# Two attention-and-FFN pairs prepared by halves of their heads, in a fused Trainium2 kernel with a fixed instruction order

## The chip, the cores and the metric

The kernel runs on one core of one Trainium2 chip. The metric is the time of the whole program on the device, in microseconds, as the median of several executions. A separate, profiled execution gives the trace and the profile page that this document reads. A core has a matrix engine (TensorE, PE in the profile; its weight loads are the row PEld), a vector engine (VectorE, DVE), a scalar engine (ScalarE, ACT), a general engine (GpSimd, POOL) and a sync engine (SyncE, SP) that issues most transfers.

## The reference, cut to what matters

Attention over four batches, eight heads, 768 positions and 64 values per head is followed by a gated feed-forward block. Three heads (0, 2 and 6) see all earlier keys; the other five see only four sink keys and a window of 64.

```python
scores = scale * q @ k.T                      # per batch and head, 768 x 768
keep   = causal & (retrieval_head | is_sink | in_window)
a      = softmax(where(keep, scores, -1e9))
x      = (a @ v) with heads side by side      # 3072 x 512
g      = x @ w_gate                           # 512 x 1536
out    = (g * sigmoid(g) * (x @ w_val)) @ w_out
```

Inputs and outputs are float32; the kernel computes its matrix products in float16 with float32 sums.

## The kernel before

The sequence is cut into 24 tiles of 128 queries, two tiles to a pair, twelve pairs. For each pair the kernel loads Q, K and V (512 KB each), casts Q and K to float16, turns them with PE transposes into a PSUM tile, and copies that tile out into `qT` and `kT`; later pairs (from the sixth on) are turned by DMA instead. Then each tile has a few score units (`sc`), an exponential for each (`ex`), the product with V (`val`), a division (`rc`, `nm`), and a transpose into `xt` (`xtr`, `xe`). Four tiles make a group, and each group has twelve column blocks of gate and value products (`gate`, `vals`), with a tanh on ACT and two instructions on DVE between them (`stt1`, `stt2`), and an output product (`out`).

Everything is a task with a name, the engines that may do it, and what it depends on. The order of all tasks and the engine of each are not found at run time: they are two long strings in the source, one for the order and one for the choices. Numbers from 3700 on in the order string are fillers: so many 512-column matmuls of the identity into a spare bank, whose result nobody reads.

```python
RINGS = {"raw": 14, "hq": 2, "e": 6, "xb": 3, "xt": 2, "sig": 2, "sil": 3,
         "h": 2 * NJ, "osb": 2, "gv": 3, "o": 1, "sc": 1, "av": 1, "tr": 1}
# "gv", "o", "sc", "av" and "tr" are PSUM; "tr" and "gv" tiles are one bank each

def recast(task, dst, src):              # float32 -> float16
    if task.way == "DVE":
        nc.vector.tensor_reduce(out=dst, in_=src.unsqueeze(len(src.shape)), ...)
    else:
        copy(task, dst, src)             # ACT or POOL

def cast(n, kd, x):                      # x is None from the third pair on
    r = landed[kd, n].rearrange("p (h j d) -> p h j d", j=2, d=64)
    ...
    if kd == "k":
        ks = slice(0, 2) if x is None else slice(x, x + 1)
        recast(T_c[n, kd, x], hqs[n][1][:, ks]..., r...[:, ks])
        return
    js = slice(0, 2) if x is None else slice(x, x + 1)      # odd or even rows
    recast(T_c[n, kd, x], hqs[n][0]...[:, :, :, js], r[:, :, js]...)

def transposes(n, w):                    # w: 0 for Q, 1 for K; eight transposes
    ring = "gv" if w and n < 2 else "tr"
    tr = buf(ring, [128, 4, 2, 2, 64] if w else [128, 2, 4, 128], FH, "tr")
    for j in range(2):
        for p in range(4):
            nc.tensor.transpose(...)
    trs[n, w] = tr

# ... for pairs 0 and 1, the copies of one PSUM tile in parts:
cut = [slice(2, 4), slice(0, 2)] if n < 2 else [slice(0, 4)]

def tasks_of_tile(t):
    ...
    k_deps = [x for kt in range(i // 2 + 1) for x in T_ev[QP.index((b, kt)), 2]]
    k_deps += T_ev[n, 0] + T_ev[n, 1]    # a score unit waits for all the parts
    for u, unit in enumerate(units):
        sc = P.add(f"sc{t}.{u}", ["PE"], ..., deps=k_deps + k_sinks + added,
                   takes=[score_ring(t, u)])
```

In the order string of this kernel the first loads are Q0, K0, Q1, V0, K1, Q2, V1, K2, then weights: two column blocks of the gate matrix (its second, then its first), and one of the value matrix.

Of the kernel before, what the change touches and what calls it, by code (L numbers as in the profile page):

```python
# [13 lines left out]


ORDER = (
    "080400091L1O021M1N01xh1T1U1W1V1Xxi1Y1a1Z1K0B0A1Rxm1t1u25261P0C280E031Q2D1r2G1S1s271n1d1o1b2E2j2I"
    "2F1e2H1i1c1f2K1p0D1q292A2J2L1g0F1y2p2k1h1j2M2C2r2q1v0j1w1k151x2V2Wxh2N1z202O2P0i0p1l2B1m2X2Z2a23"
    "242b2Yxh2Q2s9Z2R2S2c2t2T2d210H2U9j11309k312e9l109F0o2h2u9G162i9o9a9H9c2v0I0k0G9b9d3Q059e062x9f9p"
    "9q9m3W2y369n3D3Y9K0q9g22072z129I3E3X9J2f9N9L9M3A3B3M3R3Z3a9O189h2l2m9t9u9i2w3e9v9y0K329P333f9z9r"  # L20
    "9s34A00n350t3b2n37199w9x2o3C0m3cA13F3G1H3H3IA249134FAN3J4G9QAO9R3h9S9T3i3K1IAQ3g3pAP1E3z0s401FAS"
    "4HAR3d9UAV0J3S3TATAUAW3N9V3t380l3L3VAI0L9W3u1BAL3vAJ393j3k3l3mAKA8AM4A410N3n9X3o0r0O9Y3q4I423wA9"
    "3xA34o0M3U434J44ADAA4N3r4p3y3sAG453OAEAF0Q2g1CA44O4K4WABAH4q463P4L4BA54748A64Z4aBQ4MACA70xBTBR4c"
    "4l4dAwAx4vBS4CBU4xBf4PBg4DAyBh4Q4RBVBWAzBXB0ArAsB14bAtBiBj4S4w4TB24y5253B3B44U4VBGBH4z50B5BJBL5V"
    "0RBI4f0w5WBY4X4E4hBK5X1AB64gB75D4e5G5H0v17BZ1D510yB80u14BkAX5J4iB9BA0zBl4Y4j1J5K5fAY0PBM1GBNBm55"
    "4m564r54BaBEAZAa4k5L5d4s594t4u575A5cAu585B5E5eBb5g5hAvAc0T5CAdBc0bAe5I5Q5MBO0SBP5Z0UBB5N5O5RAfBC"
    "BDAhBd5P0VAi5S5TAjAb5oBFAk5pBnBeAg625Y634n64Bo5FAmAn5iAo5UCJ6761ApCd7SCKCL5r5s5tCeCf6BCgCh6ACsBp"
    "Bq5q5a68COCtCu5j7T5k695yAq656F5bCv5u7Q0X6i5v6GCPCQAlBr0W6g6CBs0a6O6p5w5x6DCwC95lCACB6ECMBuCR6UCS"
    "BvCNBwCn6V6I6hCoCpCb0Z6J6oBx6qBt0Y5zCY6kCZCaCcCT6X665m6Y6nBzCi6K6R6S7P0e6HC0C1Cl6LCjCkCmCCCUCV6M"
    "6d7W6uCD0g6T5n6v6NCE6P6w7XC260CHCxCFCGCI6rC46s7N6mC5Cy6z706Z6aCW6jCXCz6W6b6xCqC36QD08a6y7x6c6fCr"  # L30
    "6eC6C7By7O7VD2757U6tD37RD1787971D5D47AEF72E0E1E20c73D67B7C0hD7EDD876EGC87j7kEHEIEJEAEBECD9DA7D7g"
    "7t8i7l0d7vDRDB82DgDC7hEE7i7E7477DhDiE37m7n7z7FE5DSDTE6DDDEDF837GE47wE8Db7H6l7uE7E98eDUDVDcEK7I7Y"
    "7JENELEM7qEO7Z7aDHDIDd7KDe7LDq80817o0fDrDs7p877rDfDJ7yDKDWDXDYDt7b7cDu88DlDm847sDo8GDnDp857d8ZDv"
    "Dw8A7e8BDx89Dy8Y7MDM8JDG8KDjDzDk8LDN8MDZ7fEoEp8NFDFEDa868V8CFG8D8P8Q8c8E8gEqEjFFDOFH8dDPEkFIElDL"
    "EmFJ8f8h8pFL8FFKFMF88H8REP8qF9FA8jEn8k8bEQ8SEyEzFBERFC8m8lESETFS8xF0Et8nF18OEu8T8U9394F2EvEUEV8I"
    "ErEw8W8t8X90FTFUFcEW8oEx918r8uFdFe92FfEXDQ8sFX8v8wFg8y98EZFYEYEaFZ9996EsF3F495F58zEbEc979AF6FN9B"
    "9C9DEeEfF7FOFPFaFbFVEgFW9EGGEhGJEiGHGIGKGkGlGuGvGnGwGmFhFQGoGxGyFRG6G7FiFjFkFlEdG8GVGWGYGXGaG9Gb"
    "GcGZFmGpFnGqGrG1G2GAG3GsGBGtGCGdGeGDFoGLGMFpG4G5GQFrGRGSFsGTFtGOFuGNGfGgFvGPFqFwGhGEGFFxFyFzG0GU"
    "GiGzGjH0H1H4H2H3H5H6H7H8H9HAHBHEHFHCHDHGHHHJHIHKHL"
)  # L40
WAYS = (
    "000000000000000000000000000000000000000000000000000000000000002020222122002102002000012221100010"
    "001000000000100000000000000000101221222020011101100000000000000000000110022100001101001000000000"
    "100000100000000000002222220000100000100000000010000100100000000002022220110100000100000020000000"
    "100000010012202210000001001000000000100000010000000002221202000000000000000001000010022211210000"
    "000000000000220000001000000110202022000000000000000000000000000000000000012122000000000000000000"
    "010000210002221100000000010000001200010010000002001120011000000000000000000210000000000000000000"
    "000000000000000000000000000000000000000000000000000000000000000000000000000000000000000000000001"
    "000000000000000000000000000000000000000000000000000000000000000000000100001000000000000000000000"
    "000000000000000000000000000000000000000000000000000000000000000100000000000000000000000000000000"  # L50
    "000000000000000000000000000000000000010000100001000000000000000000000000000000000000000000000000"
    "000000000000000000000100000000000000000000000000000000000000000000000000000000000000000000000000"
    "10000000001000000010"
)
DIGITS = "0123456789ABCDEFGHIJKLMNOPQRSTUVWXYZabcdefghijklmnopqrstuvwxyz"

# [49 lines left out]
def kernel(  # L106
# [270 lines left out]
    def cast(n, kd, x):  # L377

        r = landed[kd, n].rearrange("p (h j d) -> p h j d", j=2, d=64)
        if n >= XQK and kd == "q":  # L380
            recast(T_c[n, kd, x],
                 hqz[:, :, x, :, x * 64:(x + 1) * 64].rearrange(
                     "p j (r k) d -> p k r j d", r=2),
                 r.rearrange("p (k s r) j d -> p s k r j d", r=2, s=2)[:, x])
            return
        if n not in hqs:
            h = buf("hq", [128, 2, 1024], FH, "hq")
            hqs[n] = [h[:, 0].rearrange("p (j r x) -> p j r x", j=2, r=2),
                      h[:, 1].rearrange("p (k a x) -> p k a x", k=2, a=4)]
        if kd == "k":  # L390
            ks = slice(0, 2) if x is None else slice(x, x + 1)
            recast(T_c[n, kd, x],
                 hqs[n][1][:, ks].rearrange("p k a (s d) -> p k s a d", s=2),
                 r.rearrange("p (k s r) j d -> p k s (r j) d", r=2, s=2)[:, ks])
            return
        js = slice(0, 2) if x is None else slice(x, x + 1)
        recast(T_c[n, kd, x],
             hqs[n][0].rearrange("p j r (k d) -> p k r j d", d=64)[:, :, :, js],
             r[:, :, js].rearrange("p (k r) j d -> p k r j d", r=2))

    def castv(n, m, j):
        b, pi = QP[n]
# [22 lines left out]

    trs = {}

    def transposes(n, w):

        ring = "gv" if w and n < 2 else "tr"  # L430
        tr = buf(ring, [128, 4, 2, 2, 64] if w else [128, 2, 4, 128], FH, "tr")
        for j in range(2):
            for p in range(4):
                if w:
                    nc.tensor.transpose(tr[:, p, :, j, :], hqs[n][1][:, p // 2, p % 2 * 2 + j],
                                        ident)
                else:
                    nc.tensor.transpose(
                        tr[:, j, p, :],
                        hqs[n][0][:, j, p // 2, (p % 2) * 128:(p % 2 + 1) * 128], ident)  # L440
        trs[n, w] = tr

    def evacq(n, s, x, ps):
        c = slice(s * 64, s * 64 + 64)
        copy(T_ev[n, s][x], qT[n % 2][c, s, ps].rearrange("c p j n -> c j p n"),
             trs[n, 0][c, :, ps])

    def evack(n, x, ps):


        b, pi = QP[n]
        copy(T_ev[n, 2][x],
             kT[b % 2][:, 2 * pi:2 * pi + 2].rearrange("c m k r x -> c (k r) m x")[:, ps],
             trs[n, 1][:, ps].rearrange("c p m j n -> c p m (j n)"))

    def sinks_k(b, m):

# [166 lines left out]
    def tasks_of_pair(n):  # L624
# [35 lines left out]
                deps=cs["k"] + older)) for m in range(2)]  # L660
            P.uses(first, "hq", *T_ev[n, 2])
        for w in range(xqk, 2 - xk):
            ring = "gv" if w and n < 2 else "tr"
            tr = P.add(f"tr{n}.{w}", ["PE"], (lambda n=n, w=w: transposes(n, w)),
                       deps=cs["qk"[w]], takes=[ring], after=[T_warm])
            cut = [slice(2, 4), slice(0, 2)] if n < 2 else [slice(0, 4)]
            evs = []
            if w:
                for x, ps in enumerate([slice(1, 4, 2), slice(0, 4, 2)] if n < 2 else cut):
                    evs.append(P.add(f"evk{n}.{x}", ["ACT", "DVE"],  # L670
                                     (lambda n=n, x=x, ps=ps: evack(n, x, ps)),
                                     deps=[tr] + older))
                T_ev[n, 2] = evs
            else:
                oldq = [x for t in (2 * n - 4, 2 * n - 3) if n > 1 for x in T_sc_of[TILES[t]]]
                T_ev[n, 0], T_ev[n, 1] = [], []
                for x, ps in enumerate(cut):
                    for s_ in range(2):
                        T_ev[n, s_].append(P.add(
                            f"evq{n}.{s_}{x}", ["ACT", "DVE"],  # L680
                            (lambda n=n, s_=s_, x=x, ps=ps: evacq(n, s_, x, ps)),
                            deps=[tr, T_fill0] + oldq))
                        evs.append(T_ev[n, s_][-1])
            P.uses(tr, ring, *evs)
            P.uses(first, "hq", tr)

    def tasks_of_tile(t):
        b, i = TILES[t]
        units = plan(t)
        n = t // 2  # L690
        k_deps = [x for kt in range(i // 2 + 1) for x in T_ev[QP.index((b, kt)), 2]]
        k_deps += T_ev[n, 0] + T_ev[n, 1]
        v_deps = [x for kt in range(i + 1) for x in T_v[QP.index((b, kt // 2)), kt % 2]]
        v_deps += [T_fill1]
        k_sinks = [T_sk[b, m] for m in range(1, i)]
# [5 lines left out]
        for u, unit in enumerate(units):  # L701
# [1 line left out]
            streams = any(kt < 0 or kt == i for p, hh, c, kt in mms if p)  # L703
            added = [T_masks[0 if t == 0 else 1]] if t < LEAD else []
            sc = P.add(f"sc{t}.{u}", ["PE"], (lambda t=t, u=u, unit=unit: scores(t, u, unit)),
                       deps=k_deps + k_sinks + added, takes=[score_ring(t, u)])
            T_sc_of[b, i].append(sc)
            if streams:
                own.append(sc)
# [223 lines left out]
```

The softmax here doesn't subtract the row's maximum and nothing guards it: scores larger than these inputs give would overflow.

## Time and profile before

| | before |
|---|---|
| time, median of 3 | 257.31 us (257.23 to 257.92) |
| span of the profiled execution | 255.5 us |
| PE busy | 246.7 us, 97% |
| DVE, ACT, POOL busy | 177.1, 135.3, 81.5 us |
| granted PE clock | 1.00 |
| filler matmuls of 512 columns | 21 |
| first gate product starts | 21.4 us |
| last matmul ends | 251.7 us |

The profile page has the busy time of each engine; the span in 40 slices; the transfers; the chain of work that ended last, which is followed back from the last instruction; and the costliest groups of instructions, with the idle time of the engine before them and what ended that idle time. The trace can also be asked for a timeline of one engine, and for a table of busy times by stretch. In a timeline each row is: start, duration, engine, source line, operation, what is written and read, shapes, how many instructions are merged into the row, and in brackets the idle time before it and what released it. Matmuls are pipelined: the 0.38 us of one 512-column matmul is its latency, and in a run of them one starts every 0.216 us (8 in 1.73 us). A busy PE is therefore not yet a PE at its peak, and 97% says little about what is left to win.

### The profile page before, as it was taken

How to read it: one execution, taken by the hardware profiler on the slowest of the kernel's cores; microseconds unless marked ns; L12 is line 12 of the kernel's file. 1: busy time of each engine (PE TensorE's matmuls, PEld its weight loads, DVE VectorE, ACT ScalarE, POOL GpSimd, SP SyncE). 2: the span in 40 equal slices, each digit the busy share in tenths (PEclk: the TensorE clock that was granted, in tenths of full speed). 3: DMA queues.
4: the chain of work that ended last, by engine and by line, in shares of the span. 5: the costliest groups of instructions: out<-in, count | busy, mean ns of one | idle time of the engine just before them, and what ended most of it. 6: DMA issues, size and time to landing. Idle time of an engine off the chain costs nothing.

```text
span 255.5 us, 4847 instructions
## 1 busy us (share of the span) xinstructions
PE 246.7 (97%) x1812; PEld 136.7 (54%) x1812; DVE 177.1 (69%) x360; ACT 135.3 (53%) x214; POOL 81.5 (32%) x118
## 2 busy tenths in 40 slices
PE   7889899999999999999999999999999999999994
PEld 3567765665555554545555555555555554444442
DVE  3777899997897566859976587778557766463511
ACT  3767998766488445645555663637753412322100
POOL 4674888695674412410450230342000100000000
PEclk9999999999999999999999999999999999999999
DMA  7999999996999958998959947254022211300444
GB/s 188 290 310 326 318 337 316 304 212 136 388 181 223 295 140 158 266 167 189 224 114 204 239 91 165 44 116 92 0 62 64 62 23 41 82 0 0 100 96 99
DMA packets 80536, 42.53 MB, mean 166 GB/s; under 512 B 32768, under 2 KB 76032, under 8 KB 80512
## 3 DMA queue, kind: packets, MB, share of 16 engines
q1 hardware_dynamic: 80352, 42.09, 68.8%
q8 instruction: 14, 0.23, 0.4%
q10 hardware_dynamic: 160, 0.13, 0.2%
q14 instruction: 10, 0.08, 0.1%
HBM read 28.31 MB, written 6.29 MB: 135 GB/s over the span
## 4 chain that ended last, share of the span: by engine, by line
PE 84%; DVE 6%; DMA 3%; ACT 3%; SPq 2%; issue 1%; POOL 1%; DVEq 0%; POOLq 0%; ACTq 0%
PE gv L778 44%; PE o_ps L813 24%; PE sc L547 9%; PE av L577 5%; DMA raw<-in_k_dram 3%; ACT e L557 2%; SPq L317 2%; DVE h L795 1%; DVE sil L788 1%; DVE xb L594 1%; DVE vt L181 1%; DVE e L565 1%; ACT qT L175 1%; DVE qT L177 1%; PE xtr L610 1%
## 5 line engine op out<-in xcount | busy, mean ns | idle before, releaser
L557 ACT ACTIVATE e<-sc 128x1024 f16<-128x1024 f32 (+3 forms) x71 | 62.2, 878 | 32.1 <-PE sc L547 31.3
L778 PE MATMUL gv<-xt,wv_sb 128*128 128x512 f16 (+1 forms) x304 | 73.5, 368 | 0.4 <-DVE sil L788 0.3
L778 PE MATMUL gv<-xt,wg_sb 128*128 128x512 f16 (+1 forms) x304 | 73.0, 368 | 0.0
L784 ACT ACTIVATE sig<-gv 128x512 f32<-128x512 f32 (+1 forms) x76 | 43.0, 574 | 51.1 <-PE gv L778 49.4
L813 PE MATMUL o_ps<-wo_sb,h 128*128 128x512 f16 (+2 forms) x300 | 69.5, 370 | 0.0
L788 DVE SCALAR_TENSOR_TENSOR sil<-sig,gv 128x512 f32<-128x512 f32 (+1 forms) x76 | 49.3, 654 | 25.1 <-ACT sig L784 24.0
L795 DVE SCALAR_TENSOR_TENSOR h<-sil,gv 128x512 f16<-128x512 f32 (+1 forms) x76 | 49.3, 654 | 20.3 <-PE gv L778 18.9
L813 PEld LDWEIGHTS <-h 128*128 128x128 f16 x300 | 28.5, 98 | 30.0
L778 PEld LDWEIGHTS <-wg_sb 128*128 128x128 f16 x304 | 28.8, 98 | 27.2 <-issue 0.2
L778 PEld LDWEIGHTS <-wv_sb 128*128 128x128 f16 x304 | 28.7, 98 | 25.9 <-issue 0.6
L547 PE MATMUL sc<-qT,kT 128*128 128x256 f16 (+1 forms) x276 | 37.4, 257 | 0.5 <-ACT e L557 0.5
L565 POOL TENSOR_TENSOR e<-e,m 128x640 f16<-128x640 f16 (+1 forms) x16 | 26.3, 1641 | 33.9 <-ACT e L557 32.2
L547 PEld LDWEIGHTS <-kT 128*128 128x128 f16 x276 | 24.6, 98 | 12.3 <-issue 1.3
L577 PEld LDWEIGHTS <-e 128*128 128x128 f16 x472 | 19.6, 97 | 11.1 <-DVE xb L594 2.2
L577 PE MATMUL av<-vt,e 128*128 128x65 f16 x472 | 22.0, 193 | 1.3 <-DVE xb L594 0.5
L175 ACT COPY o_sb<-o_ps 128x512 f32<-128x512 f32 (+1 forms) x14 | 8.1, 578 | 26.0 <-PE o_ps L813 26.0
L594 DVE TENSOR_TENSOR xb<-av,rc 128x256 f16<-128x256 f32 x47 | 19.9, 424 | 1.6
L177 POOL CAST vt<-raw 64x512 f16<-64x512 f32 x24 | 15.5, 644 | 16.0 <-DMA raw<-in_v_dram 14.9
L177 POOL CAST hq<-raw 128x1024 f16<-128x1024 f32 (+1 forms) x15 | 14.2, 947 | 15.7 <-DMA raw<-in_k_dram 14.4
L177 POOL COPY vt<-vt 2x330 f16<-2x330 f16 x14 | 6.3, 453 | 37.6 <-PE av L577 37.3
L582 DVE RECIPROCAL rc<-av 128x4 f32<-128x4 f32 x48 | 8.5, 177 | 10.4 <-PE av L577 10.1
L565 DVE TENSOR_TENSOR e<-e,m 128x1024 f16<-128x1024 f16 (+1 forms) x22 | 14.7, 668 | 0.8 <-ACT e L557 0.8
(58 smaller groups left out, 130.9 us busy)
## 6 DMA issues: line engine op xcount, KB each, us to landing
raw<-in_q_dram SPq DMA_DIRECT2D x12, 512.0 KB, 6.5
raw<-in_k_dram SPq DMA_DIRECT2D x12, 512.0 KB, 7.0
raw<-in_v_dram SPq DMA_DIRECT2D x12, 512.0 KB, 7.0
out_dram<-o_sb SPq DMA_DIRECT2D x46, 128.0 KB, 2.4
raw<-in_moe_w_gate_dram SPq DMA_DIRECT2D x6, 512.0 KB, 7.8
raw<-in_moe_w_val_dram SPq DMA_DIRECT2D x6, 512.0 KB, 7.9
raw<-in_moe_w_out_dram SPq DMA_DIRECT2D x6, 512.0 KB, 6.7
xt<-xb SPq DMA_TRANSPOSE x16, 2.4
```

The lines of the kernel that those rows point to most:

```text
L175: nc.scalar.copy(out=dst, in_=src)
L177: ENG[task.way].tensor_copy(out=dst, in_=src)
L547: nc.tensor.matmul(sc[c // 4][:, c % 4:c % 4 + n, :], weights, moving, start=first, stop=last)
L557: nc.scalar.activation(out=e[:, 0:n], in_=whole_sc.pop((t, u))[:, 0:n], func=AF.Exp, scale=scale)
L565: ENG[task().way].tensor_tensor(out=ev, in0=ev, in1=mm, op=ALU.mult)
L577: nc.tensor.matmul(av[:, n, 0:65], ee, vv, start=(m == 0), stop=(m == len(bl) - 1))
L594: nc.vector.tensor_tensor(out=xbs[t][:, :, odd, :], in0=av[:, :, 0:64], in1=rc.to_broadcast([128, 4, 64]), op=ALU.mult)
L778: nc.tensor.matmul(ps, wsb[:, kk, j * 128:(j + 1) * 128], xt[:, kk, c[0]:c[1]], start=(kk == 0), stop=(kk == 3))
L784: nc.scalar.activation(out=sg[g, j, c], in_=gs[g, j, c], func=AF.Tanh, scale=0.5)
L788: nc.vector.scalar_tensor_tensor(out=sl[g, j, c], in0=sg.pop((g, j, c)), scalar=1.0, op0=ALU.add, in1=gs.pop((g, j, c)), op1=ALU.mult)
L795: nc.vector.scalar_tensor_tensor(out=hs[g, j][:, c[0]:c[1]], in0=sl.pop((g, j, c)), scalar=0.5, op0=ALU.mult, in1=vs.pop((g, j, c)), op1=A ...
L813: nc.tensor.matmul(o_open[g, tt, x], hs[g, j][:, tt * 128:(tt + 1) * 128], wo_sb[:, j, lo:hi], start=(j == 0), stop=(j == NJ - 1))
```

## The change

For the first two pairs, cast, transpose and copy are cut by the same line: the pairs of heads whose scores are needed together. Half 0 is the head pairs (1, 3) and (5, 7), half 1 is (0, 2) and (4, 6). Before, Q's casts were cut by odd and even rows and K's by another index, so a transpose of either half of the heads needed both casts; all eight transposes of Q or of K went into one PSUM tile; and every score unit waited for all copies. Now each half has its own cast, its own four transposes, its own PSUM tile (one in the `tr` ring, one in the `gv` ring) and its own copies, and a score unit waits only for the halves that it reads. The loads stay whole, 512 KB each. The purpose is that the first scores need not wait for the second half, and that two engines can empty two different PSUM tiles at the same time. As all dependencies near the start differ, both strings, the order and the choice of engine for every task, were planned anew for the whole kernel. The new order begins Q0, K0, Q1, K1, V0, V1, Q2, K2, then gate block 1, value block 1, gate block 0, and it has 15 filler matmuls in place of 21.

```diff
 ORDER = (
-    "080400091L1O021M1N01xh1T1U1W1V1Xxi1Y1a1Z1K0B0A1Rxm1t1u25261P0C280E031Q2D1r2G1S1s271n1d1o1b2E2j2I"
+    "000104081L1T021V1M1U1W091Oxj1b1c1N0B1X271Z1a281Yxi1p1f2I0C1q2J0A2K2A1d1e1t2N1g292L2M2O1r1Q031S1P"
 # ... both strings replaced to their ends
     def cast(n, kd, x):
+        rs = slice(0, 2) if x is None else slice(1 - x, 2 - x)
         if kd == "k":
-            ks = slice(0, 2) if x is None else slice(x, x + 1)
+            js = slice(2 * rs.start, 2 * rs.stop)
             recast(T_c[n, kd, x],
-                 hqs[n][1][:, ks].rearrange("p k a (s d) -> p k s a d", s=2),
-                 r.rearrange("p (k s r) j d -> p k s (r j) d", r=2, s=2)[:, ks])
+                 hqs[n][1][:, :, js].rearrange("p k a (s d) -> p k s a d", s=2),
+                 r.rearrange("p (k s r) j d -> p k s (r j) d", r=2, s=2)[:, :, :, js])
             return
-        js = slice(0, 2) if x is None else slice(x, x + 1)
         recast(T_c[n, kd, x],
-             hqs[n][0].rearrange("p j r (k d) -> p k r j d", d=64)[:, :, :, js],
-             r[:, :, js].rearrange("p (k r) j d -> p k r j d", r=2))
+             hqs[n][0].rearrange("p j r (k d) -> p k r j d", d=64)[:, :, rs],
+             r.rearrange("p (k r) j d -> p k r j d", r=2)[:, :, rs])
-    def transposes(n, w):
-        ring = "gv" if w and n < 2 else "tr"
-        tr = buf(ring, ...)
+    def transposes(n, w, x):
+        ps = range(4) if x is None else range(2 - 2 * x, 4 - 2 * x)
+        tr = buf(tr_ring(n, w, x), ...)
         for j in range(2):
-            for p in range(4):
+            for p in ps:
+    def tr_ring(n, w, x):
+        return "tr" if x is None or w == x else "gv"
 # ... the copies evacq and evack read the tile of their own half
-        k_deps = [x for kt in range(i // 2 + 1) for x in T_ev[QP.index((b, kt)), 2]]
-        k_deps += T_ev[n, 0] + T_ev[n, 1]
+        def k_deps(unit):
+            halves = sorted({p < 2 for p, hh, c, kt in unit[0]})
+            parts = [(QP.index((b, kt)), 2) for kt in range(i // 2 + 1)] + [(n, 0), (n, 1)]
+            return [x for m, w in parts
+                    for x in ([T_ev[m, w][h] for h in halves] if m < 2 else T_ev[m, w])]
```

## The prediction, made before the changed kernel was run

> **What bounds the kernel now.** I read the page's engine busy times first, then the chain of waits, then busy time by stretch, and last the timeline of the start and the end.
>
> ```profile
> PE 246.7 (97%) x1812; PEld 136.7 (54%) x1812; DVE 177.1 (69%) x360; ACT 135.3 (53%) x214; POOL 81.5 (32%) x118
> ...
> PE 84%; DVE 6%; DMA 3%; ACT 3%; SPq 2%; issue 1%; POOL 1%; DVEq 0%; POOLq 0%; ACTq 0%
> ```
>
> The chain that ended last is 84% PE, so PE's work bounds it, and all else is 16%. How much of PE's time is work? The groups by shape have 823 useful matmuls of 512 columns, 14 of 384, 270 of 256, 212 of 128 and 472 of 65: 553,688 columns. Eight of 512 take 1.73 us in the chain, 0.422 ns a column: 233.9 us. The last matmul ends at 251.7, so 17.8 us are lost before it. Adding up the columns of the rows of PE's timeline shows where. At 6 us nothing useful is done (6.0 lost); at 12 us 7,296 columns, 3.1 us of work (8.9 lost); at 24 us 26,288, 11.1 us (12.9 lost); at 60 us 103,950, 43.9 us (16.1 lost). The remaining 190 us lose 2 us more.
>
> ```profile
> core 0: us, PE busy (x) PEld busy (x) DVE busy (x) ACT busy (x) POOL busy (x), PEclk, DMA share, GB/s
> ...
> 6.00:12.00 6.00, 5.61 (x51) 3.86 (x50) 4.03 (x7) 4.08 (x9) 3.51 (x9) 1.00 1.20 290
> 12.00:24.00 12.00, 10.18 (x135) 7.83 (x135) 9.31 (x29) 8.24 (x17) 7.54 (x12) 1.00 1.15 316
> 24.00:40.00 16.00, 15.17 (x150) 11.20 (x148) 14.51 (x38) 14.99 (x24) 13.80 (x17) 1.00 1.13 326
> 40.00:60.00 20.00, 19.51 (x188) 12.18 (x186) 18.51 (x43) 14.19 (x22) 13.40 (x17) 1.00 1.02 251
> ```
>
> Columns are the stretch, its length, then busy time (instructions) of PE, PEld, DVE, ACT and POOL. Two regimes are to be seen. Up to 24 us transfers run full and no engine is full: work waits for data and for a chain over DVE, ACT and POOL. From 24 to 60 us DVE is busy 33.0 of 36 us, so DVE sets PE's pace. The change aims at the first regime.
>
> ```profile
> 6.74 0.69 DVE L181 TENSOR_REDUCE hq<-raw 128x512 f16<-128x512 f32 x1 [3.46 <-DMA raw<-in_k_dram]
> ...
> 7.01 0.58 ACT L175 COPY qT<-tr 64x512 f16<-64x512 f16 x1 [0.94 <-PE tr L438]
> ...
> 7.62 0.42 DVE L177 COPY qT<-tr 64x512 f16<-64x512 f16 x1 [0.19 <-ACT qT L175]
> ...
> 8.07 1.06 ACT L175 COPY qT<-tr 64x512 f16<-64x512 f16 x2 [0.48 <-DVE qT L177]
> ```
>
> Here ACT copies, DVE copies, ACT copies again, each released by the other: four copies of one PSUM tile in a row, 7.01 to 9.13.
>
> **What the Trainium skill says.** "PSUM — Partial Sum Buffer", section on bank collisions: no two engines may access the same bank at once in the same partitions, two reads included, and software must order them. The rows above agree: the copies never overlap. Two tiles in two banks lift that between the halves, not within one. "Perfetto Trace Analysis", section on optimizing Scalar/DVE operations: each instruction has a fixed cost, yet breaking one up may let work be completed sooner. The trace: a DVE copy of 64x512 takes 0.42 us, of 64x1024 0.69. But here the casts and copies were halves already, so no such cost is added. "TensorE: Matmul & The Clock Gate", section on what is actually happening: the array starts at half clock and speeds up after about 3.4 us of sustained work. The fillers agree: 0.43 us apart until 6 us, 0.21 apart at 6.81. Six fillers fewer might threaten that; I see no gap of even 1 us in PE's new order before 16 us, so I expect full clock.
>
> **The change part by part.**
>
> *Removed and added.* Per pair there are still four casts, sixteen transposes and six copies of the same sizes. Six fillers go (6 x 0.216 = 1.3 us), but they stood in waits, so I count 0.
>
> *First scores, up to 14 us.* A walk through the new order with durations of the rows before. Transfers keep their places in the queue, so data come at 4.9, 6.7, 8.5, 10.4, 12.1, 13.9, 15.8, 17.6 (from the casts that waited for them), now as Q0, K0, Q1, K1, V0, V1, Q2, K2. Q0's halves are now cast on POOL, whose mask work ends at 3.54 + 1.41 (five instructions that stood after a cast at 7.33 to 8.74) = 4.95; casts 0.61 each, to 6.2. Half of the transposes, DVE copy 0.42 and ACT copy 0.58 give 7.3; K0's casts end at 7.4 (DVE) and 7.9 (ACT, after its copy); transposes 0.4 and copies 0.4 to 0.6 give 9.0. First scores: 9.0 against 9.23. The four copies are no longer in a row, but K's cast on ACT (7.3 to 7.9, a wait for the copy) takes the place of the wait. V0 now lands fifth, at 12.1, so the first value product is at 12.3 + 0.69 (cast on DVE) + 0.1 = 13.1, against 13.77. Gain so far 0.2 to 0.7.
>
> *14 to 24 us.* DVE now has, from V0's cast to the last division of tile 2, 28 instructions in one row: two V casts (0.69), five copies of Q and K (0.42 or 0.69), eight `rc` (0.18), eight `nm` (0.42), three `xe` (0.42) and two small sink copies, 10 us in all, and summed with their waits from 12.3 to about 22.8. Before, ACT did one division, one V cast and one `xe` of these. So the first gate product comes after 21.9 against 21.38, though with more attention done (scores 4.0, value 3.0 and one `xtr` are ahead of it). By 24 us I count in the new order: transposes 6,144 columns, masks 5,376, scores of tiles 0 to 3 6,144 and of tile 4 1,408, values 3,120, `xtr` 2,048, two gates 2,048: 26,288, the same as before. It could be there 0.5 us sooner, but the next gate product needs gate block 0, now eleventh in the queue, at 23.5 in place of 21.9, and its cast 0.6. Sum for this stretch: 0 (from 0.5 faster to 0.5 slower).
>
> *24 to 31 us.* The same walk on: the 0.91 us `hqz` memset, at 8.7 before, stands at 23.4 in DVE's way; gate product 0.4.0 waits 0.9 us for its weights' cast on POOL (28.3). By 31.2 I count 40,880 columns; before, 38,064 by 30 and 48,824 by 35, which puts 40,880 near 31.6. Gain 0.4, as uncertain as its size.
>
> *31 to 60 us.* Tasks that leave DVE up to the first gate of the second group: six casts, two copies (0.42 + 0.69), three masks (0.58 + 0.71 + 0.71), two sink copies of V (2 x 2 x 0.48) and four `xe` (0.42 each), 6.7 us without the casts. Tasks that come: six casts, two copies (0.84), two masks (1.42), one `nm` (0.42), one sink copy (0.96), one `xe` (0.42), one weight cast (1.20): 5.3 us. DVE is 1.4 us lighter where it is the bound; PE lost 16.1 - 12.9 = 3.2 us from 24 to 60. I take a third, 0.5.
>
> *60 to 250 us.* PE is busy throughout but for one gap of 0.17 at 118; nothing to gain. 0, give or take 0.4.
>
> *The end.*
>
> ```profile
> 251.13 0.48 ACT L175 COPY o_sb<-o_ps 128x384 f32<-128x384 f32 x1 [3.95 <-PE o_ps L813]
> 251.65 1.39 ACTq L834 DMA_DIRECT2D out_dram<-o_sb  x2
> 251.82 0.29 DVE L177 COPY o_sb<-o_ps 128x128 f32<-128x128 f32 x1 [1.98 <-PE o_ps L813]
> ```
>
> ACT copies 384 columns, then issues two stores (1.39 us for both), while DVE copies the last 128. In the new choices ACT does the last copy too, and it stands behind the first store's issue: 251.65 + 0.56 (the first of the two issues) + 0.05 = 252.3 against 251.82. That is 0.45 later, of which the old second issue at 252.3 hides a part: copy 0.28 plus 0.07, so 0.35 us slower.
>
> Sum: 257.3 - 0.4 - 0.5 + 0.35, and 0 for the rest: **256.8 us**.
>
> **The rivals.** *DVE's row from 12 to 23 us is the new wait*, in place of the shared PSUM tile: DVE is already busy 9.31 of 12 us there, and the new order gives it more. If my sum is short by 1 us, all of it goes to PE: 257.8. Against it: copies are pipelined by 0.07 us, which I counted only in part. *Transfers bound the start anyway*: by 17.6 us the eight attention loads have landed in either order, weights after, so halves can only shift waits. Then front and start give 0, and only the middle and the end are left: 257.2. For it: 290 to 316 GB/s throughout. *The halves really free the start*: if PE has 1.5 us more done by 24 us and keeps it, 255.7. Against it: the weights that land at 21.9 and 23.5. *The clock falls back* for want of fillers: several us at half clock, 259; the granted clock stayed at 1.00 before, and the gaps are small.
>
> **Range and chances.** The walk is good to about 0.7 us, the middle to 0.5 and the rest to 0.4: about 1 us together, and a replanned order is more apt to meet unforeseen waits than gifts. I take 255.5 to 258.2. 2% would be 5.1 us; all that is lost from 6 to 24 us is 6.9, so faster or slower by that much each get 0.01.
>
> **What would show it.** Right: first transposes near 5.7 with Q0 cast on POOL; copies on ACT and DVE of the two tiles overlapping; first value product near 13.1; about 26,300 useful columns by 24 us; DVE nearly without a gap from 12 to 23 us and the first gate near 22; the last ACT copy behind a store issue, and 0.3 us more from the last matmul to the end. Wrong: a column count at 24 us off by more than 2,400 (1 us), loads that land in other places, fillers above 0.22 us apart after 8 us, or a new gap of PE after 60 us, which I did not follow through the order.

## The result, and the profile after

| | before | changed |
|---|---|---|
| time, median of 4 runs each on one chip | 257.56 us (257.23 to 257.92) | 259.32 us (258.79 to 259.65) |
| span of the profiled execution | 255.5 us | 257.9 us |
| PE, DVE, ACT, POOL busy | 246.7, 177.1, 135.3, 81.5 us | 246.1, 169.2, 140.4, 95.1 us |
| useful columns begun by 24 us | 26,288 | 26,288 |
| last matmul ends | 251.7 us | 253.6 us |
| last matmul to the end of the span | 3.76 us | 4.29 us |

The changed kernel is slower: ratio 1.0066, 95% interval 1.004 to 1.0093. The prediction was 256.8 with a range of 255.5 to 258.2, so it missed, and on the wrong side.

Engine busy times and the chain of waits, of the changed kernel:

```profile
PE 246.1 (95%) x1806; PEld 136.2 (53%) x1806; DVE 169.2 (66%) x336; ACT 140.4 (54%) x220; POOL 95.1 (37%) x133
...
PE 74%; DMA 9%; SPq 6%; DVE 5%; ACT 2%; POOL 1%; issue 1%; ACTq 0%; POOLq 0%; DVEq 0%
```

DVE is busy 8 us less than before and POOL 14 us more. The chain is 74% PE in place of 84%, with 9% of transfers. That share is misleading: the chain follows the last releaser at each step, and where it runs over transfers (mostly up to 22 us and from 78 to 95 us) PE was losing little more than before. What PE lost, the time less its useful columns at 0.422 ns, is the better guide: 12.9 us by 24 us in both kernels; 14.1 against 13.9 by 30 us; then 16.9 against 15.4 by 45 us, 17.9 against 16.15 by 60 us, and the same 1.8 to 1.9 us apart when the last matmul ends. The loss lies **between 30 and 50 us**.

Busy time by stretch, columns as in the table that the prediction shows:

```profile
core 0: us, PE busy (x) PEld busy (x) DVE busy (x) ACT busy (x) POOL busy (x), PEclk, DMA share, GB/s
6.00:12.00 6.00, 5.39 (x48) 3.17 (x46) 4.28 (x9) 4.59 (x9) 0.76 (x2) 1.00 1.20 290
12.00:24.00 12.00, 9.86 (x130) 7.51 (x129) 9.88 (x30) 8.60 (x14) 6.36 (x11) 1.00 1.15 316
24.00:40.00 16.00, 14.33 (x148) 10.90 (x147) 15.20 (x34) 14.56 (x24) 13.28 (x17) 1.00 1.13 317
40.00:60.00 20.00, 18.70 (x188) 12.14 (x186) 16.75 (x38) 15.78 (x24) 16.99 (x22) 1.00 0.82 221
```

From 24 to 40 us DVE is busy 15.20 us with 34 instructions, where before it was busy 14.51 us with 38: fewer instructions that take longer. Rows of the changed kernel's timeline show which:

```profile
29.80 1.40 POOL L571 TENSOR_TENSOR e<-e,m 128x640 f16<-128x640 f16 x1
...
30.32 1.42 DVE L571 TENSOR_TENSOR e<-e,m 128x1024 f16<-128x1024 f16 x1
...
35.34 1.04 POOL L177 CAST hq<-raw 128x1024 f16<-128x1024 f32 x1
...
35.59 1.33 DVE L571 TENSOR_TENSOR e<-e,m 128x1024 f16<-128x1024 f16 x1
...
37.01 1.04 POOL L177 CAST hq<-raw 128x1024 f16<-128x1024 f32 x1 [0.63 <-DMA raw<-in_k_dram]
37.17 0.67 DVE L802 SCALAR_TENSOR_TENSOR h<-sil,gv 128x512 f16<-128x512 f32 x1
...
37.30 1.02 PE L785 MATMUL gv<-xt,wg_sb 128*128 128x512 f16 x4 [0.27 <-DVE sil L795]
...
38.01 2.12 POOL L571 TENSOR_TENSOR e<-e,m 128x1024 f16<-128x1024 f16 x1
38.10 2.38 DVE L571 TENSOR_TENSOR e<-e,m 128x640 f16<-128x640 f16 x1
```

DVE multiplies exponentials by a mask (`e<-e,m`). With POOL idle that takes 0.68 us for 1024 columns and 0.48 us for 640 (medians of the same rows elsewhere in both traces). At 35.59 and 38.10 it takes 1.33 and 2.38 us, and each time a POOL instruction is running that began just before. DVE's ends a fixed time after POOL's: 36.92 is 0.54 us after 36.38; 40.48 is 0.35 us after 40.13. The one at 30.32 takes 1.42 us behind a POOL multiplication that ends at 31.20 (0.54 us after it again). So DVE is shown as busy, but it is waiting: 3.3 us in these three, 0.66 us in one such case of the same stretch in the kernel before. Not every DVE instruction is held: `h<-sil,gv` reads `sil` from SBUF and `gv` from PSUM; at 37.17 it runs beside POOL's cast and takes 0.67 us, and with or without POOL at work its 128x512 form takes 0.67 to 0.69 us in this whole trace. And what stands behind it comes late: PE's product at 37.30 had to wait for `sil`, which DVE made right after the multiplication of 35.59.

The Trainium skill has this: "SBUF — State Buffer", section "Who interferes with whom", says that a DVE instruction with two SBUF inputs contends with a GpSimd instruction that reads SBUF, that the pair of ports is an exclusive lock, and that the later one to issue waits until the first has finished. The waits in these rows agree with it, with ends 0.54 or 0.35 us after POOL's each time; the ports themselves no trace here shows. The prediction did not use it.

PE's waits of the changed kernel from 24 to 60 us (total, times, longest):

```profile
PE av L583 <- DVE xb L600: 0.9, 2, 0.8
PE gv L785 <- POOL wg_sb L177: 0.9, 2, 0.6
PE gv L785 <- DVE h L802: 0.5, 1, 0.5
PE gv L785 <- DVE sil L795: 0.3, 1, 0.3
```

These are the four longest. Three are on DVE; the other is for weights that POOL casts, and the kernel before has no such wait there. And among the 25 longest pieces of the chain that ended last, one is DVE's multiplication itself:

```profile
38.18 2.30 DVE e L571
```

### The profile page after: what moved, and what is told of

Its sections match the earlier page's. It is cut to its first block, busy times and chain, and to the rows that moved or that the text cites. A ratio compares the mean times of both kernels' runs of the same rounds, so it can differ in the third digit from the quotient of the medians.

```text
span 257.9 us, 4831 instructions
## 1 busy us (share of the span) xinstructions
PE 246.1 (95%) x1806; PEld 136.2 (53%) x1806; DVE 169.2 (66%) x336; ACT 140.4 (54%) x220; POOL 95.1 (37%) x133
## 4 chain that ended last, share of the span: by engine, by line
PE 74%; DMA 9%; SPq 6%; DVE 5%; ACT 2%; POOL 1%; issue 1%; ACTq 0%; POOLq 0%; DVEq 0%
PE gv L785 42%; PE o_ps L820 21%; PE sc L553 7%; SPq L317 4%; PE av L583 4%; DMA raw<-in_moe_w_val_dram 3%; DMA raw<-in_k_dram 3%; DMA qT<-hqz 2%; DVE e L571 2%; DVE m L255 1%; DMA out_dram<-o_sb 1%; DVE h L802 1%; DVE sil L795 1%; SPq L325 1%; ACT e L563 1%
## 5 line engine op out<-in xcount | busy, mean ns | idle before, releaser
L563 ACT ACTIVATE e<-sc 128x1024 f16<-128x1024 f32 (+4 forms) x71 | 62.1, 879 | 33.4 <-PE sc L553 31.9
L785 PE MATMUL gv<-xt,wv_sb 128*128 128x512 f16 (+1 forms) x304 | 72.4, 368 | 0.1
L820 PE MATMUL o_ps<-wo_sb,h 128*128 128x512 f16 (+2 forms) x300 | 68.5, 370 | 0.0
L571 POOL TENSOR_TENSOR e<-e,m 128x1024 f16<-128x1024 f16 (+1 forms) x21 | 37.4, 1785 | 35.1 <-ACT e L563 34.7
L175 ACT COPY o_sb<-o_ps 128x512 f32<-128x512 f32 (+2 forms) x16 | 8.9, 559 | 27.4 <-PE o_ps L820 26.4
L177 POOL COPY vt<-vt 2x330 f16<-2x330 f16 x22 | 10.0, 453 | 37.5 <-PE av L583 35.3
L177 POOL CAST hq<-raw 128x1024 f16<-128x1024 f32 (+1 forms) x13 | 12.4, 958 | 8.9 <-DMA raw<-in_k_dram 8.4
L571 DVE TENSOR_TENSOR e<-e,m 128x1024 f16<-128x1024 f16 (+1 forms) x17 | 13.7, 808 | 1.1 <-ACT e L563 1.0
```

The lines of the kernel that those rows point to most:

```text
L177: ENG[task.way].tensor_copy(out=dst, in_=src)
L563: nc.scalar.activation(out=e[:, 0:n], in_=whole_sc.pop((t, u))[:, 0:n], func=AF.Exp, scale=scale)
L571: ENG[task().way].tensor_tensor(out=ev, in0=ev, in1=mm, op=ALU.mult)
L785: nc.tensor.matmul(ps, wsb[:, kk, j * 128:(j + 1) * 128], xt[:, kk, c[0]:c[1]], start=(kk == 0), stop=(kk == 3))
L820: nc.tensor.matmul(o_open[g, tt, x], hs[g, j][:, tt * 128:(tt + 1) * 128], wo_sb[:, j, lo:hi], start=(j == 0), stop=(j == NJ - 1))
```

## The experiments

Theory: **the hold-up**. The new plan puts more of POOL's work (21 multiplications in place of 16, and casts) beside DVE's multiplications, and DVE, which sets PE's pace from 24 to 60 us, waits. Rivals: the halves themselves cost time; the new plan simply gives DVE the wrong load or order; a memset of 0.91 us that moved into the busy stretch; the end.

In the table, "held" is what DVE's multiplications took from 30 to 60 us above 0.683 us (1024 columns) or 0.481 us (640), in the one profiled execution. "Lost" is what PE lost from 24 to 60 us in it. Each time is a median with its ratio to the kernel before on the same chip.

| kernel | time, us | ratio | held, us | lost, us |
|---|---|---|---|---|
| before | 257.4 to 257.6 | 1 | 0.7 | 3.2 |
| changed | 259.32 | 1.0066 [1.004, 1.0093] | 3.3 | 5.0 |
| 1 halves, old plan | 257.40 | 1.0007 [0.9998, 1.0017] | 0.6 | 3.2 |
| 2 no halves, new plan | 259.03 | 1.006 [1.0046, 1.0074] | 1.7 | 4.0 |
| 3 changed, two masks from POOL to DVE | 258.89 | 1.0061 [1.0049, 1.0073] | 1.3 | 4.4 |
| 4 changed, three masks replaced | 257.55 | 1.0005 [0.9995, 1.0015] | 0 | 3.1 |
| 5 changed, memset early | 259.25 | 1.0063 [1.0043, 1.0083] | 1.3 | 3.3 |
| 6 changed, last copy on DVE | 258.72 | 1.005 [1.0033, 1.0067] | 3.2 | 4.8 |
| 7 before, one mask moved | 256.73 | 0.997 [0.9958, 0.9982] | 0 | 2.6 |
| 8 before, one mask replaced | 256.74 | 0.997 [0.9956, 0.9984] | 0.4 | 3.1 |
| 9 before, the mask moved the other way | 257.94 | 1.0014 [1.0003, 1.0024] | 1.7 | 4.0 |
| 10 changed, 3 and more together | 258.26 | 1.0033 [1.0015, 1.005] | 0 | 3.3 |
| 11 halves, old plan, mask moved as in 7 | 256.97 | 0.9978 [0.9965, 0.999] | 0 | 2.6 |

One profiled execution need not be typical of the median. That of the changed kernel was the slowest of four (259.65 us); those of 2, 3, 5 and 10 were the fastest of theirs (258.73, 258.50, 257.54 and 257.64 us); those of 8 and 9 took 257.17 and 258.20 us. Nor does "lost" follow "held" one for one: with 1.3 us held, 5 lost 0.2 us more than 4.

### 1. Halves with the old plan

The changed kernel with the order and the engines of the kernel before; a task that was split takes the place and the engine of the one that it came from.

```diff
-ORDER, WAYS = the new plan
+ORDER, WAYS = the old plan, split tasks side by side   # one copy of Q moved ahead of K's second transposes
```

> The changed code (halves of the heads, own PSUM tiles, score units that wait for their own half) with the order and the engine choices of the kernel before, carried over name by name; each half tile is transposed where the whole one was. Theory lock (the loss lies in the new plan, where DVE's mask multiplications meet POOL instructions): the halves cost nothing, 257.3 to 257.8 us, within 0.3 of before, and the multiplication at about 38 us is the only one held up. Rival halves (the finer cut itself costs): about 259, as the changed kernel.

257.40 us, the same as before. Useful columns by 24 us are 26,288 once more, and the first matmuls of the scores start at 9.17 us against 9.23. The copies no longer take turns, but that moved nothing. The halves cost nothing and, in this order, bring nothing: the new plan is what is slow.

### 2. The new plan without the halves

```diff
-ORDER, WAYS = the old plan
+ORDER, WAYS = the new plan, split transposes joined again
```

> The kernel before, without the halves (casts, transposes and copies cut as before), with the changed kernel's order of tasks and choice of engines carried over. The other side of the run that gave the changed kernel the old order (257.40). New-plan theory: it meets the same three hold-ups of DVE's mask multiplications in 30 to 41 us (2 to 3.3 us together) and takes 258.5 to 259.6. Halves theory, or halves and plan only together: 257.2 to 257.8.

259.03 us: the new plan alone costs what the changed kernel costs. Two things in its trace matter. By 24 us PE has lost 13.7 us in place of 12.9, so in the new order the halves do start the work 0.8 us earlier. Yet the time is no worse for it. The rows of DVE and POOL say why:

```profile
35.32 1.04 POOL L177 CAST hq<-raw 128x1024 f16<-128x1024 f32 x1
...
36.28 0.68 DVE L565 TENSOR_TENSOR e<-e,m 128x1024 f16<-128x1024 f16 x1
...
37.89 2.12 POOL L565 TENSOR_TENSOR e<-e,m 128x1024 f16<-128x1024 f16 x1
38.14 2.21 DVE L565 TENSOR_TENSOR e<-e,m 128x640 f16<-128x640 f16 x1
```

POOL's cast stands where it stood, at 35.3, as it follows data that land. DVE, 0.7 us later than in the changed kernel, reaches its multiplication at 36.28, 0.08 us before POOL is through, and goes free. So does the one of 31.33. Of the three hold-ups that were expected only the last is there, for 1.73 us. Being early at 24 us moved the changed kernel's DVE into POOL's way.

### 3. Fewer multiplications on POOL

```diff
-mask4.1: POOL   mask6.0: POOL
+mask4.1: DVE    mask6.0: DVE
```

> The changed kernel with two mask multiplications, mask4.1 and mask6.0, on DVE in place of POOL; nothing else moves. Theory lock: the DVE multiplications at 30.3 and 38.1 us, 1.42 and 2.38 us long while POOL multiplied, fall to about 0.68 and 0.48; DVE gains 2.6 us of waiting and takes on 1.2 us of work; PE loses about 1 us less from 28 to 50 us; 258.2 to 258.6 in all. Rival load (DVE has too much to do there, and two more multiplications make it worse): 259.6 to 260.3.

258.89 us. DVE has two more multiplications, 1.2 us of work, and the kernel did not become slower, so the load theory, which asked for 259.6 us or more, is out. But the gain is about 0.1 by the ratios and at most 0.4 by the medians, less than the hold-up theory said. The trace shows what was overlooked: with POOL's multiplications gone, DVE's met POOL's casts, one held for 0.86 us and one for 0.41. It also shows the lock the other way round:

```profile
39.95 1.61 POOL L179 CAST wg_sb<-raw 128x1024 f16<-128x1024 f32 x1 [1.77 <-DMA raw<-in_moe_w_gate_dram]
...
39.99 0.68 DVE L573 TENSOR_TENSOR e<-e,m 128x1024 f16<-128x1024 f16 x1
```

DVE runs at full speed and POOL's cast, 1.04 us by itself, takes 1.61: here POOL waited, though its recorded start is 0.04 us the earlier. In the same execution a POOL cast that began at 35.70 led DVE's multiplication at 35.74 by the same 0.04 us, and there DVE waited (1.54 us). So recorded starts as close as this do not tell who waits.

### 4. The same list, without the second operand

The multiplications of tile 4 unit 0 and tile 5 units 0 and 1 are left out, so their masks are not applied. In the place of each stands a DVE instruction of 512 or 320 elements that reads one operand from SBUF and rewrites it. Everything else stays, POOL's work too.

```diff
-tensor_tensor(out=ev, in0=ev, in1=mm, op=mult)
+tensor_reduce(out=half, in_=half.unsqueeze(3), axis=X, op=max)   # half: every second column of ev
```

> The changed kernel, order and engines untouched, but three mask multiplications on DVE (tile 4 unit 0, tile 5 units 0 and 1; those that took 1.42, 1.33 and 2.38 us) are left out and in the place of each stands a DVE instruction of about the length that the multiplication has when POOL reads nothing (0.69 and 0.50 us), which reads only one operand from SBUF. DVE's list keeps its length and its load; only the second operand is gone. Hold-up theory: the three take 0.69, 0.69 and 0.50 us even beside POOL's multiplications and casts, DVE is 3.2 us lighter in 30 to 41 us, PE has lost about 16.4 us by 60 us (17.9 before this edit, 16.15 in the kernel before the change), and the time falls by 1.2 to 1.8 us, to 257.5 to 258.1. Load theory (the plan gives DVE too much to do or in a bad order): the time stays at 259.0 to 259.6.

```profile
35.20 0.72 DVE L575 TENSOR_REDUCE e<-e 128x512 f16<-128x512 f16 x1
35.31 1.04 POOL L177 CAST hq<-raw 128x1024 f16<-128x1024 f32 x1
...
36.99 1.04 POOL L177 CAST hq<-raw 128x1024 f16<-128x1024 f32 x1 [0.63 <-DMA raw<-in_k_dram]
37.06 0.51 DVE L575 TENSOR_REDUCE e<-e 128x320 f16<-128x320 f16 x1
```

257.55 us, at the low end of what the hold-up theory said, and no longer distinguishable from the kernel before. DVE and POOL now run through each other without either growing longer. Order, engines and the length of DVE's list are those of the changed kernel, so neither load nor order explains what comes back here, about 1.6 us by the ratios. PE's last matmul ends at 251.6 us, as in the kernel before (251.7); the end is as long as in the changed kernel. PE's waits on `xb` and `sil` from 24 to 60 us fall from 1.2 to 0.3 us; those on `h` (0.5) and on the weights that POOL casts (0.7) stay, so they belong to the new plan and not to the hold-up. The replacement also has half as many elements; that the second SBUF operand is what counts rests on `h<-sil,gv` above as well.

### 5 and 6. Two smaller suspects

The 0.91 us memset of `hqz`, which stands at 24.3 us in the changed kernel's DVE, put at the beginning where DVE is idle:

```diff
-... fill3 (DVE) behind the first group's divisions
+... fill3 (DVE) ahead of the first copy of Q
```

> The changed kernel with the 0.91 us memset of the DMA-transposed Q buffer moved from 24.3 us, where DVE sets the pace, to the start, where DVE waits for Q. Theory lock: DVE's work moves 0.8 us earlier, but the multiplications are still held up until POOL's instruction ends, so most of it is swallowed: 258.9 to 259.4. Rival load: all of it comes back, 258.4 to 258.6.

259.25 us: the memset is not the cause. The six executions ran from 257.54 to 259.5. The profiled one was the fastest, and of its three multiplications one was not held at all (35.50, 0.68 us) and one for 0.57 us only. So the same program, with starts some tenths of a microsecond earlier or later, is held more or less; the other five have no trace.

The last copy of 128 columns, back on DVE:

```diff
-oe5.3.1: ACT
+oe5.3.1: DVE
```

> The changed kernel with the last copy (128 columns) on DVE as in the kernel before, in place of ACT, where it stands behind the issue of a store. From the last matmul to the end took 4.29 us changed and 3.76 before: expected 0.4 to 0.5 us less, 258.8 to 258.95. If the tail is set by something else, such as the landing of earlier stores, no change, 259.3.

258.72 us, within a spread of 257.77 to 259.45 that is too wide to measure a few tenths, so the trace decides. The last store lands 2.67 us after the last matmul, against 2.85 in the changed kernel and 2.68 before, so what the copy cost came back, 0.18 us. The rest of the 0.53 us by which the end is longer did not: 1.43 us pass between the landing and the end of the span in place of 1.08, in the exchange of semaphores that closes the program, where POOL pauses for 0.3 to 0.4 us. That pause stands in every profiled run with the new plan and in none with the old one; why, stays open.

### 7, 8 and 9. The same lever in the kernel before

If the hold-up is the cause, the one of 0.66 us in the kernel before must be worth something too. In its DVE and POOL rows:

```profile
38.14 1.04 POOL L177 CAST wv_sb<-raw 128x1024 f16<-128x1024 f32 x1 [0.67 <-DMA raw<-in_moe_w_val_dram]
38.38 1.14 DVE L565 TENSOR_TENSOR e<-e,m 128x640 f16<-128x640 f16 x1
```

Moved ahead of one DVE instruction, it falls into the 0.67 us in which POOL waits for data:

```diff
-... stt2 0.4.0, mask5.1 ...
+... mask5.1, stt2 0.4.0 ...
```

> The kernel before with one DVE multiplication (tile 5 unit 1, 1.14 us at 38.38, of which 0.66 us lie beside POOL's cast of a weight block) moved ahead of the instruction before it, into the 0.66 us in which POOL waits for data. Hold-up theory: it takes 0.48 us, DVE is 0.6 us lighter at 38 us, and a third to a half of it comes out: 256.9 to 257.2, faster than both kernels by a little. Rival: PE is not held by DVE at that place, 257.3 to 257.5.

```profile
36.55 1.04 POOL L184 CAST hq<-raw 128x1024 f16<-128x1024 f32 x1
...
37.81 0.49 DVE L572 TENSOR_TENSOR e<-e,m 128x640 f16<-128x640 f16 x1
38.18 1.04 POOL L184 CAST wv_sb<-raw 128x1024 f16<-128x1024 f32 x1 [0.59 <-DMA raw<-in_moe_w_val_dram]
```

256.73 us, **faster than both kernels**, by 0.65 us for one swap of two neighbours (256.65 to 256.82 in six executions). It gained more than the third to a half of 0.6 us that was expected.

Was it the new order of the two, or the hold-up? The order kept, and that one multiplication left out (its mask is not applied), with a one-operand instruction of 0.51 us in its place:

```diff
-tensor_tensor(out=ev, in0=ev, in1=mm, op=mult)
+tensor_reduce(out=half, in_=half.unsqueeze(3), axis=X, op=max)   # tile 5, unit 1 only
```

> The kernel before with the order untouched, but DVE's multiplication of tile 5 unit 1 (1.14 us at 38.38, beside POOL's cast of a weight block) left out, and in its place a DVE instruction of about 0.50 us that reads one operand from SBUF. The run that moved this multiplication gained 0.65 us and mixed two things, another order and no hold-up; here the order stays. Hold-up theory: DVE is 0.6 us lighter at 38 us and the time is 256.6 to 256.9. If the new order was what paid: 257.2 to 257.5.

256.74 us, the same gain with the order untouched. The profiled execution took 257.17 us, and in it another multiplication, at 43.67, was held for 0.41 us by a POOL cast that began 0.06 us before it.

And the other way, to where POOL is in the middle of its own multiplication:

```diff
-... stt2 0.3.256, stt1 0.5.0, nm4.0, sv0.2, stt2 0.4.0, mask5.1 ...
+... mask5.1, stt2 0.3.256, stt1 0.5.0, nm4.0, sv0.2, stt2 0.4.0 ...
```

> The kernel before with the same multiplication moved the other way, ahead of the third instruction before it and its neighbours, to about 35.0 us, where POOL's own multiplication runs until 36.5. Same work, same engines. Hold-up theory: it takes 36.5 - 35.0 + 0.35 = 1.85 us (1.14 before, 0.48 alone) and DVE is 0.7 us heavier than in the kernel before: 257.7 to 258.4. Order theory: an earlier multiplication does no harm, 257.2 to 257.5.

```profile
34.82 2.13 POOL L572 TENSOR_TENSOR e<-e,m 128x1024 f16<-128x1024 f16 x1
...
36.00 1.30 DVE L572 TENSOR_TENSOR e<-e,m 128x640 f16<-128x640 f16 x1
```

257.94 us, slower than before by about 0.4 us. The multiplication was held for 0.82 us and not for 1.37, because DVE came there 1 us later than expected: an earlier one, at 30.18, had been held for 0.84 us by a POOL cast that began at 30.13. Together 1.66 us, 1.0 more than before. The one at 30.18 stands ahead of everything that was moved, so the move did not cause it, and this execution took 258.20 us. The same instructions on the same engines thus take 256.73, 257.4 to 257.6, or 257.94 us, by where one of them stands.

### 10 and 11. Put together

The changed kernel with the two masks of 3 on DVE, one of DVE's multiplications moved ahead of a division so that it starts before POOL's cast of K, and the last copy on DVE:

```diff
-mask4.1: POOL   mask6.0: POOL   oe5.3.1: ACT   ... nm4.0, ex6.0, mask5.0 ...
+mask4.1: DVE    mask6.0: DVE    oe5.3.1: DVE   ... mask5.0, nm4.0, ex6.0 ...
```

> The changed kernel with what the earlier runs pointed to, together: two POOL mask multiplications (tile 4 unit 1, tile 6 unit 0) given to DVE, DVE's multiplication of tile 5 unit 0 moved ahead of one division so that it starts before POOL's cast of K and not beside it, and the last copy of 128 columns on DVE. Hold-up theory: excess of DVE's multiplications in 30 to 41 us falls to about 0.4 us (3.3 in the changed kernel, 1.3 with the first edit alone), PE has lost about 16.7 us by 60 us, and with 0.2 us less at the end the time is 257.6 to 258.2, still no better than the kernel before. Load theory: DVE has two multiplications more, 259 or above.

258.26 us, by the ratios 0.8 us better than the changed kernel, slower than the kernel before, and just above the expected 257.6 to 258.2. In the profiled execution all five multiplications between 30 and 40 us take 0.48 to 0.68 us, with none held. The others, up to 259.1 us, have no trace, so what they met is not known.

The halves with the old plan and the swap of 7:

```diff
-... stt2 0.4.0, mask5.1 ...      # in the kernel of 1
+... mask5.1, stt2 0.4.0 ...
```

> The halves (the changed kernel's code) with the old order and the one move that gained 0.65 us in the kernel before. If the halves are worth nothing in the old order (257.40 against 257.35 there): 256.6 to 256.9, no different from the kernel before with the same move (256.73). If the halves' earlier copies were hidden behind the hold-up: below 256.5.

256.97 us, just above what was expected, and not distinguishable from 7 by the intervals; in the profiled executions PE has lost 15.5 us by 60 us in both. The halves again bring nothing in this order.

## Why the prediction was wrong, step by step

*The start, up to 24 us: right.* First transposes at 5.64 (predicted 5.7), first score products at 9.10 (9.0), first value product at 13.19 (13.1), first gate product at 22.46 (after 21.9), 26,288 columns by 24 us (26,288). The copies of different tiles do overlap, as these rows of the changed kernel show:

```profile
8.27 0.41 DVE L177 COPY qT<-tr 64x512 f16<-64x512 f16 x1
8.46 0.59 ACT L175 COPY kT<-tr 128x512 f16<-128x512 f16 x1 [0.49 <-PE tr L435]
8.60 1.26 DVE L181 TENSOR_REDUCE hq<-raw 128x512 f16<-128x512 f32 x2
9.06 0.58 ACT L175 COPY qT<-tr 64x512 f16<-64x512 f16 x1
```

The granted clock stayed at 1.00. (At the very start, fillers of the kernel before are still 0.43 us apart at 5.61, 4.2 us after the first, a little longer than the 3.4 us that the prediction quotes.) Of the rivals, "the halves really free the start" is refuted, and so is "the clock falls back". "DVE's row is the new wait" did not come true either: DVE was busy 9.88 of 12 us there and no time was lost. Nor was it nearly without a gap from 12 to 23 us, as one of the signs had it: it was busy 9.11 of 11 us. "Transfers bound the start anyway" foresaw the same 0 for the start, so the count cannot tell it from the prediction; run 2, where joining the halves again in this order costs 0.8 us by 24 us, shows that transfers alone do not set the start.

*24 to 31 us, gain 0.4: missed by about half a microsecond.* By 30 us PE had lost 14.1 us against 13.9. The 40,880 columns that were expected by 31.2 us were begun at 31.70, against 31.56 before. So it was level or 0.2 us behind. The wait for weights that was foreseen came, 0.64 us at 28.45 in place of 0.9.

*31 to 60 us, gain 0.5: the step that failed.* It said "DVE is 1.4 us lighter where it is the bound". It counted DVE's instructions by their durations in rows where POOL did not disturb them, and took what POOL does at the same time as free. Even the row that would have warned, 1.14 us for a multiplication that took 0.48 elsewhere, was in the profile of before. DVE was indeed busy less in 24 to 60 us, 31.95 us in place of 33.02, but 3.3 us of that was three multiplications standing still. From 24 to 60 us PE lost 5.0 us in place of 3.2: 1.8 us worse, where these two steps promised 0.9 better. Experiment 4 brings this back to 3.1 us with only these three replaced. Nor was there a gain behind it. With no multiplication held in either, the new plan lost 3.1 us there (4) and the old one 2.6 (7), so the third of 1.4 us that was taken as gain shows nowhere.

*60 to 250 us, 0 within 0.4: right.* 1.78 us apart at 60 us and 1.86 at the last matmul. In between, at 96 to 97 us, just behind the place where the chain runs over transfers, the changed kernel fell 0.6 us further behind, and by 130 us it had taken that back. PE waits 0.42 us there for an exponential: the new gap after 60 us that the prediction named among the signs of being wrong, but it did not last.

*The end, 0.35 slower: right in its mechanism, not in its size.* As predicted, the last copy stands behind a store's issue:

```profile
252.95 0.48 ACT L175 COPY o_sb<-o_ps 128x384 f32<-128x384 f32 x1 [1.32 <-PE o_ps L820]
253.46 0.56 ACTq L841 DMA_DIRECT2D out_dram<-o_sb  x1
254.05 0.27 ACT L175 COPY o_sb<-o_ps 128x128 f32<-128x128 f32 x1 [0.63 <-PE o_ps L820]
254.35 0.50 ACTq L841 DMA_DIRECT2D out_dram<-o_sb  x1
```

It starts 0.47 us after the last matmul, against 0.09 before. But the stores land only 0.17 us later, and 0.36 us came from the closing exchange, which the sum did not have: 0.53 in all.

*The range.* It allowed 1 us of error and named "unforeseen waits" as the likelier side, yet its upper end lies only 0.9 us above the kernel before. It had DVE as the bound from 24 to 60 us, so a wait of DVE itself would come out in good part, and none was in the sum. Of the changed kernel's 3.3 us held PE lost 1.9 (against run 4); of the 0.66 us in the kernel before it lost all (against run 7).

## What to carry to other kernels

Before moving work to an idle engine, ask what it shares with the engine that is the bound: here POOL reading SBUF stops DVE's multiplications of two SBUF operands, so POOL's 14 us more were not free. In a profile, look at the longest and the shortest duration of one instruction in one shape; where they differ, find what ran on the other engine, as an engine shown as busy may be waiting. A fixed order can be mended by swapping neighbours so that such an instruction falls into a gap of the other engine (0.65 us here), or an instruction that reads one operand from SBUF can take its place where the program allows that (runs 4 and 8 show the time of it, but leave masks out).

## What the runs showed that was not expected

- A held multiplication ends 0.54 us (1024 columns) or 0.35 us (640 columns) after POOL's instruction does, within 0.02 us in all 48 held cases of the thirteen traces. That is its time alone (0.68 and 0.48) less about 0.14 us: some of it seems to be done while it waits.
- POOL can be the one that waits (1.61 us for a cast of 1.04), and recorded starts 0.04 us apart went either way: in run 3 POOL's lead of 0.04 us won at 35.70 and lost at 39.95. So executions of one program differ in what they meet. How much of their spread (257.54 to 259.5 us in run 5) comes from it is not shown: those of run 11, whose profiled one has none held before 60 us, spread too, from 256.65 to 258.46.
- More progress at the start can cost time later: POOL's casts follow landed data, DVE's multiplications follow progress, and 0.8 us earlier at 24 us moved one into the other. That it cost the whole 0.8 us is argued from the trace of run 2, not tested by itself.
